# Loading wv in whole rows between the x chunks, both halves of V per row block, and first statistics on two engines

## The chip, the cores and the metric

The kernel runs on one core of a Trainium2 chip. The metric is the device time of one execution in microseconds, about 1.25 us more than the span from the first to the last instruction in its trace (795.23 against 794.0 in the profiled run of the kernel before). Each run also comes with the mean clock that TensorE was granted over its span; here this matters more than usual, since a clock of 0.998 over 795 us is some 1.6 us, and the whole effect of the change is smaller than that.

Engines are named as in the profile: PE is TensorE's matmul, PEld its weight load, DVE VectorE, ACT ScalarE, POOL GpSimd, SP SyncE, which issues the loads.

## The reference, cut to what matters

```python
x = A_x                                         # 2048 x 1024, bf16
h = x + A(layernorm(x), wq, wk, wv, wo, beta)   # attention with a memory, in 4 segments of 512 rows
out = h + B(layernorm(h), w_in, w_sp, b_sp, w_out)
# first thing in A:  v = layernorm(x) @ wv      (1024 x 1024 weights), then q and k the same way
```

The change touches only the first 22 of some 794 us: layernorm of the first 512 rows (four chunks of 128), their transposes, and the first 56 matmuls of `v`.

## The kernel before

Operations are collected in a program; a list scheduler with its own cost model then fixes the order on every engine but TensorE, whose order is that of the source. The parts that matter:

```python
LOAD = "12ab3h"          # x1, x2, wv rows 0-3 left half, rows 4-7 left half, x3, wv right half
START = 'T00 t01 v00 v01 v02 v03 t10 T11 v04 v05 v06 v07 v10 ... v27 u00 u01 ... u27 v30 ... v37'
# Tci / tci: transpose half i of x chunk c on TensorE, copy out of PSUM by VectorE (T) or ScalarE (t)
# vci / uci: matmul of chunk c with row block i of wv, left (v) or right (u) half of the columns
...
def wv_rows(a, b):       # half rows: 512 columns of bf16, 1 KB each
    dma(WV[:, a:b, 0:512], A_wv.rearrange("(c p) n -> p c n", p=128)[:, a:b, 0:512])
...
for k in range(N_WARM):  # 11 matmuls on zeros while the first loads are under way
    mm(PS[:, 7, :], ZERO[:, 0:128], ZERO[:], True, True)
...
def layernorm_act(src, dst, junk, k):            # chunk 1: both statistics on ScalarE, all 1024 columns
    e.activation(junk, src, Identity, scale=-1/D, accum_out=nm)
    e.activation(junk, src, Square, bias=nm, accum_out=ss)
    ...
# chunks 0, 2, 3: two bn_stats of 512 columns each on VectorE, bn_aggr,
# then for all: square root on ScalarE, reciprocal and normalising on VectorE
```

The softmax here doesn't subtract the row's maximum and nothing guards it: scores larger than these inputs give would overflow.

## Time and profile before

| | kernel before |
|---|---|
| time, median of the first 3 runs | 795.27 us (795.21 to 795.57) |
| span of the profiled run | 794.0 us, clock 1.000 |
| TensorE busy | 782.5 us |
| first matmul of V | 8.24 us |
| first matmul of Q (wq) | 21.29 us |

The two last rows are start times counted from the start of the span.

The prediction below shows the waits, the chain and TensorE's timeline. What the other engines do up to the first matmul of V is in their timelines (start, duration, engine, line, operation, output and input; in brackets the idle time and what ended it):

```profile
5.13 1.06 ACT L585 ACTIVATE hx<-xin 128x1024 bf16<-128x1024 bf16 x1
...
6.31 1.15 ACT L587 ACTIVATE hx<-xin,mv 128x1024 bf16<-128x1024 bf16 x1
6.58 0.42 DVE L485 COPY xnT<-ps 128x512 bf16<-128x512 bf16 x1
...
7.79 0.58 ACT L473 ACTIVATE xnT<-ps 128x512 bf16<-128x512 bf16 x1
```

ScalarE does the two full-width statistics of chunk 1. The first copy of chunk 0 out of PSUM is done by VectorE and ends at 7.00; from there on the first matmul lacks only its weights, which land at 8.20.

### The profile page before, as it was taken

The numbers are of one execution on the slowest core, as the hardware profiler recorded it, in microseconds if no ns is written. First come the engines' busy times: TensorE is split into PE (matmuls) and PEld (weight loads), VectorE is DVE, ScalarE is ACT, GpSimd is POOL, SyncE is SP. The second block draws the span as 40 slices with busy tenths as digits, with TensorE's granted clock in tenths as the row PEclk, the third lists the DMA queues.
The fourth block names the chain that finished last, engine by engine and source line by source line (L and its number), as shares of the span: only waits on it lengthen the run. The fifth ranks groups of instructions, "written<-read, shape, count | busy, mean of one in ns | idle before, by whom it ended". The sixth has DMA issues, their size and how long they took to land.

```text
span 794.0 us, 11952 instructions
## 1 busy us (share of the span) xinstructions
PE 782.5 (99%) x5273; PEld 321.4 (40%) x4765; DVE 369.3 (47%) x854; ACT 290.7 (37%) x342; POOL 138.9 (17%) x266
## 2 busy tenths in 40 slices
PE   8999999999999999999999999999999999999999
PEld 3455554555554542341322314443244334423433
DVE  6784687868766686804215051132223222322222
ACT  5778887787878852132323323100000000000000
POOL 0454543444433431200001010000000000000000
PEclk9999999999999999999999999999999999999999
DMA  9756612732333657610000116703410530012001
GB/s 282 189 128 159 149 42 67 144 84 55 72 82 103 161 134 211 159 40 1 1 0 1 26 35 156 188 1 68 119 33 1 119 100 1 0 54 61 0 1 53
DMA packets 129526, 65.02 MB, mean 82 GB/s; under 512 B 96576, under 2 KB 121408, under 8 KB 129472
## 3 DMA queue, kind: packets, MB, share of 16 engines
q1 hardware_dynamic: 129472, 64.25, 32.4%
q8 instruction: 39, 0.64, 0.3%
q14 instruction: 15, 0.12, 0.1%
HBM read 32.51 MB, written 8.39 MB: 52 GB/s over the span
## 4 chain that ended last, share of the span: by engine, by line
PE 96%; DVE 1%; issue 1%; DMA 1%; ACT 0%; SPq 0%; POOL 0%
PE ps L327 78%; PE ps L328 15%; PE ps L464 3%; DMA wv<-in_A_wv_dram 1%; ACT e L473 0%; DVE stats L570 0%; SPq L516 0%; DVE hx L495 0%; DVE pkt L498 0%; DVE xin L489 0%; PE ps L468 0%; DVE oq L495 0%; DVE v L485 0%; POOL e L700 0%; POOL ra L505 0%
## 5 line engine op out<-in xcount | busy, mean ns | idle before, releaser
L327 PE MATMUL ps<-wspT,z 128*128 128x512 bf16 x878 | 193.1, 379 | 0.9
L473 ACT ACTIVATE e<-ps 128x2048 bf16<-128x2048 f32 x80 | 149.8, 1873 | 35.1 <-PE ps L464 35.1
L327 PEld LDWEIGHTS ps<-wspT,z 128*128 128x128 bf16 x896 | 87.7, 98 | 106.4 <-issue 1.0
L473 ACT ACTIVATE z<-ps 128x512 bf16<-128x512 f32 x120 | 63.1, 571 | 145.4 <-PE ps L327 140.5
L495 DVE TENSOR_TENSOR tg<-ps,brow 128x512 bf16<-128x512 f32 x56 | 38.7, 691 | 150.0 <-PE ps L327 121.9
L327 PE MATMUL ps<-hnT,win 128*128 128x512 bf16 x438 | 96.7, 379 | 0.5
L700 POOL TENSOR_SCALAR_AFFINE_SELECT e<-e 128x1024 bf16<-128x1024 bf16 (+1 forms) x80 | 77.4, 968 | 112.2 <-ACT e L473 111.8
L328 PE MATMUL ps<-win,hnT 128*128 128x512 bf16 (+1 forms) x381 | 90.0, 343 | 0.5
L570 DVE BATCH_NORM_STATS2 stats<-z 128x6 f32<-128x448 bf16 x64 | 40.1, 627 | 96.8 <-ACT z L473 95.2
L327 PE MATMUL ps<-wout,y 128*128 128x512 bf16 (+2 forms) x243 | 82.4, 367 | 0.0
L328 PE MATMUL ps<-wout,y 128*128 128x512 bf16 x210 | 79.6, 379 | 0.5
L495 DVE TENSOR_TENSOR hx<-hx,ps 128x512 bf16<-128x512 bf16 (+1 forms) x65 | 42.3, 674 | 77.2 <-PE ps L327 76.8
L327 PEld LDWEIGHTS ps<-hnT,win 128*128 128x128 bf16 x448 | 43.9, 98 | 54.1 <-issue 2.0
L327 PE MATMUL ps<-xnT,wq 128*128 128x512 bf16 x250 | 60.3, 380 | 0.4 <-issue 0.2
L327 PE MATMUL ps<-xnT,wk 128*128 128x512 bf16 (+2 forms) x249 | 57.4, 373 | 2.4 <-DVE ra L502 1.9
L327 PE MATMUL ps<-wv,xnT 128*128 128x512 bf16 x239 | 57.1, 379 | 2.4 <-DMA wv<-in_A_wv_dram 1.5
L327 PE MATMUL ps<-wo,oT 128*128 128x512 bf16 x244 | 57.1, 379 | 0.6
L327 PEld LDWEIGHTS ps<-wout,y 128*128 128x128 bf16 x252 | 24.2, 98 | 72.2 <-issue 69.1
L327 PE MATMUL ps<-win,hnT 128*128 128x512 bf16 x122 | 46.2, 379 | 0.0
L327 PEld LDWEIGHTS ps<-win,hnT 128*128 128x128 bf16 x128 | 12.5, 98 | 81.4 <-issue 80.9
L509 POOL TENSOR_SCALAR rs<-mv 128x1 f32<-128x1 f32 x44 | 10.9, 248 | 192.9 <-DVE mv L573 192.9
L327 PEld LDWEIGHTS ps<-v,e 128*128 128x128 bf16 x1280 | 40.1, 96 | 9.8 <-issue 1.7
(72 smaller groups left out, 635.3 us busy)
## 6 DMA issues: line engine op xcount, KB each, us to landing
win<-in_B_w_in_dram SPq DMA_DIRECT2D x6, 1024.0 KB, 5.7
hx<-in_A_x_dram SPq DMA_DIRECT2D x16, 256.0 KB, 3.3
out_dram<-hx SPq DMA_DIRECT2D x16, 256.0 KB, 2.7
hx<-out_dram SPq DMA_DIRECT2D x16, 256.0 KB, 2.6
out_dram<-hx SPq DMA_DIRECT2D x31, 128.0 KB, 1.7
xin<-in_A_x_dram SPq DMA_DIRECT2D x15, 256.0 KB, 5.0
wout<-in_B_w_out_dram SPq DMA_DIRECT2D x2, 1792.0 KB, 11.1
wq<-in_A_wq_dram SPq DMA_DIRECT2D x2, 1024.0 KB, 8.7
```

The costliest lines, as they stand in the source:

```text
L327: return e.matmul(out, lhsT, rhs, start=start, stop=stop)
L328: return e.add_instruction(mybir.InstMatmult(name="I-%d" % (1000000 + o.idx), engine=e.engine, ins=[e.lower_ap(rhs), e.lower_ap(lhsT)], ou ...
L464: G.op(PE, lambda e: e.matmul(o, lhsT, rhs, start=True, stop=True, tile_position=(32 * i, 0)), [lhsT, rhs], [o], n / 2.4 if last else 3.5, ...
L473: G.op(ACT, lambda e: e.activation(o, i, func, scale=scale, **kw), r, [o], ((172 if inps(i) else 224) + n_of(i)) / 1.2 + 26, prio=prio, na ...
L495: G.op(DVE, lambda e: e.tensor_tensor(o, a, b, op), [a, b], [o], vcost(o, [a, b], fast), name="tt", prio=late[0])
L509: G.op(POOL, lambda e: e.tensor_single_scalar(o, i, s, op), [i], [o], 220 if n_of(o) < 8 else 220 + 2.5 * n_of(o), name="pts1", prio=late[0])
L570: G.op(DVE, lambda e, si=si, so=so: e.bn_stats(so, si), [si], [so], (cs + 143) / 0.96, name="bn_stats", prio=late[0])
L700: G.op(POOL, lambda e: e.affine_select(d, d, pat, ALU.is_ge, 0.0, base=0, channel_multiplier=-1), [d], [d], 1270 if j else 640, name="mask")
```

## The change

The intent: bring the first weights in sooner by loading them in small pieces of whole rows (2 KB), between the chunks of x; give TensorE two matmuls per row block and chunk, so that few blocks keep it busy; and split the statistics of chunks 1 to 3 by columns over ScalarE and VectorE, so that the next chunk is ready in time. Two smaller edits go with it: the first copy of chunk 0 out of PSUM moves from VectorE to ScalarE (`T00` becomes `t00`), and `AFTER` now holds chunk 1's first bn_stats back until chunk 0 is normalised. In the cut below, what stands in parentheses sums up code.

```diff
-    ON_ACT = (1,)
-    LOAD = "12ab3h"
-    START = 'T00 t01 v00 v01 v02 v03 t10 T11 v04 ... (left halves, then right halves)'
-    AFTER = [(1, 1, 5)]
+    SPLIT = (0, 384, 512, 512)      # columns of each chunk's statistics on ScalarE
+    LOAD = "1 0:1 1:3 2 3:4 4:5 3 5:6 6:8"     # x1, row block 0, blocks 1-2, x2, ...
+    START = ("t00 t01 u00 u01 v00 u02 v01 T10 T11 v02 u03 v03 u10 u11 v10 v11 v12 u04 v13 v04 u12 u13 v14 v05 v15 "
+             "t20 u05 u14 v06 v16 T21 v20 u20 u21 u06 v21 v22 u15 u16 u22 v17 ... u27 v30 ... v37 ")
+    AFTER = [((1, 'b0'), (0, 'ts'))]
...
-        dma(WV[:, a:b, 0:512], A_wv.rearrange("(c p) n -> p c n", p=128)[:, a:b, 0:512])
+    dma(WV[:, a:b, :], A_wv.rearrange("(c p) n -> p c n", p=128)[:, a:b, :])
...
-    (layernorm_act for chunk 1; bn_stats of all columns for chunks 0, 2, 3)
+    def layernorm_first(c, wa):
+        ... wa columns: mean and sum of squares on ScalarE, written as one more group of bn_stats
+        ... the rest: bn_stats on VectorE; bn_aggr joins them; the tail as before
...
-        if i == 0: vb[x[:2]] = bank()
+        b = PS[:, 2 + 2 * (c % 3) + h, :]       # both halves of a chunk have their own banks
```

The cost model of the scheduler also takes whole-row loads as 8% cheaper.

## The prediction

> **What bounds the kernel now.** I read four views in this order: the page's busy shares, the waits of TensorE, the chain that ended last over the first microseconds, and the engines' timelines up to 26 us. The page first:
>
> ```profile
> PE 782.5 (99%) x5273; PEld 321.4 (40%) x4765; DVE 369.3 (47%) x854; ACT 290.7 (37%) x342; POOL 138.9 (17%) x266
> PE 96%; DVE 1%; issue 1%; DMA 1%; ACT 0%; SPq 0%; POOL 0%
> ```
>
> TensorE is busy for 782.5 of 794.0 us and carries 96% of the chain that ended last. The change does not remove a matmul, so all it can touch is 794.0 - 782.5 = 11.5 us of TensorE idleness, and only the part before attention starts: the diff changes nothing after the first projections of V. The waits and the chain show where in that start TensorE stands still:
>
> ```profile
> PE ps L327 <- DMA wv<-in_A_wv_dram: 1.5, 1, 1.5
> ...
> 2.64 5.56 DMA wv<-in_A_wv_dram
> 8.20 0.05 issue
> 8.24 1.04 PE ps L327 x4
> 9.28 0.45 PE ps L468 x8
> 9.73 2.00 PE ps L327 x9
> 11.73 0.45 PE ps L468 x8
> 12.17 0.22 PE ps L327
> 12.39 0.05 issue
> 12.44 12.49 PE ps L327 x65
> ```
>
> The start waits for the first wv load: issued at 2.64, landed at 8.20. From there on the chain is TensorE alone. The timeline of TensorE says the same, with exact starts:
>
> ```profile
> 5.91 0.89 PE L468 MATMUL ps<-ident,xin 128*128 128x128 bf16 x8
> 8.24 1.04 PE L327 MATMUL ps<-wv,xnT 128*128 128x512 bf16 x4 [1.45 <-DMA wv<-in_A_wv_dram]
> ...
> 12.01 9.44 PE L327 MATMUL ps<-wv,xnT 128*128 128x512 bf16 x42
> 21.29 1.89 PE L327 MATMUL ps<-xnT,wq 128*128 128x512 bf16 x8
> ```
>
> Between 8.24 and 21.29 there are 56 matmuls of V and two groups of 8 transposes. The 43 matmuls from 12.01 to 21.29 give 9.28 / 43 = 0.216 us each; 56 x 0.216 = 12.1, and the two groups take 9.61 - 9.11 = 0.50 and 12.01 - 11.55 = 0.46 us. The sum is 13.05 us, and 21.29 - 8.24 is 13.05 us: once it has begun, this stage has no hole at all. **What can be won is therefore how much earlier than 8.24 the first matmul of V starts, less every new hole.**
>
> **What the Trainium skill says, and whether the trace agrees.**
> "TensorE: Matmul & The Clock Gate", section "Wait — 56ns, not 53.3ns?", gives 215.7 ns from start to start at N = 512; the trace has 216 ns, so the 13.05 us cannot shrink.
> "ScalarE: Activation LUTs", section "What ACT_TABLE_LOAD costs", gives an ACTIVATE as 186 ns + 0.833 ns per column, 93 ns more with a pointer operand. The two statistics of chunk 1 (1024 columns) take 1057 and 1147 ns in the trace against 1039 and 1132: it agrees, so I use it to size the narrower ones.
> "Perfetto Trace Analysis", section "DMA Optimizations", says that pieces under 2 KB have a noticeable overhead and that splitting may let some work start sooner. The trace agrees in direction: half rows of wv and wq (1 KB) moved at 359 GB/s between 10.3 and 13.2 us, and whole rows of x (2 KB) at 392 GB/s between 20.6 and 21.3, 9% more.
> "DMA: Bandwidth & Descriptors", section "Anatomy of one DMA — SWDGE (gpsimd) path", has some 2 us fixed for a DMA on that other path; here the two small pieces of x chunk 0 landed 2.2 and 2.3 us after issue, so small pieces do not come for nothing, but they overlap.
>
> **The change part by part.**
>
> *Loads.* Before, in order: x0 (two halves), x1, x2, wv rows 0-3 left half (512 KB), rows 4-7 left half, x3, right half (1 MB), wq. The issue and landing of each give, for the bytes up to and with it: 512 KB (x1) at 5.1 us, 768 KB (x2) at 5.8, 1280 KB (first wv) at 8.2, 1792 KB at 9.5, 2048 KB (x3) at 10.3, 3072 KB at 13.2. After: x0, x1, row block 0 (256 KB, whole rows), 1-2, x2, 3, 4, x3, 5, 6-7. On the old curve row block 0 lands at 5.8, blocks 1-2 (1280 KB) at 8.2, block 3 (1792 KB) at 9.5. But the old curve was drawn with 1 KB pieces and 512 KB at a time. By the throughput instead: 0.33 MB had moved at 3.5 us, at 370-390 GB/s blocks 1-2 (1.31 MB in all) have moved by 6.1, and with the 1.2 to 1.6 us by which landings trailed the moved bytes before, they land at 7.3 to 7.7; block 3 likewise at 8.8 to 9.1. I take 7.6 and 9.0. The issues themselves cost 0.43 to 0.51 us each; eleven of them end near 6 us, ahead of the data.
>
> *Chunk 0.* Its statistics are untouched (VectorE, done at 5.84), and the transposes start at 5.91 as before. But both copies out of PSUM now go to ScalarE, where chunk 1's statistics over 384 columns stand first: they start at 5.13 as now, take 0.52 + 0.19 and 0.61 + 0.19 us (1057 and 1147 ns less 640 columns x 0.833, and the accumulator reads of 0.19), so they end at about 6.6; the copy of 0.58 ends at 7.2. The first matmul of V then starts at about 7.25, 1.0 us before 8.24. This is the ceiling of the gain.
>
> *New holes.* The first matmul uses block 0; the second needs block 1, 7.6 against 7.47: 0.15 lost. Chunk 1: VectorE takes 640 columns in two pieces (a 512-wide one takes 0.69, so about 0.48 each) from 5.84 to 6.8, aggregation 0.21, square root 0.29 behind the copy on ScalarE until about 7.45, reciprocal 0.16, normalising 0.55: ready at 8.2, and TensorE arrives at 7.6 + 4 x 0.216 = 8.5. No hole. After both transposes (0.48) and one matmul TensorE wants block 3 at 9.2; it is there at 9.0, or up to 0.3 late. From then on each block of 0.7 us of loading is met with five to eight matmuls (1.1 to 1.7 us), so the loads run ahead. Chunk 2 lands near 8.5, its two ScalarE statistics over 512 columns take about 1.7 us, its normalised rows come near 11.7, and TensorE needs them after 21 matmuls near 12.7. Chunk 3 becomes ready near 13.9 instead of 13.4; the wk load hangs on it and lands perhaps 0.5 later than the present 20.6, wanted at 22.2. Neither should hold.
>
> *Sum.* 1.0 ceiling - 0.15 for blocks 1-2 - 0.1 for block 3 - 0.1 for small things later = 0.65 us earlier at the first wq matmul. What follows is bounded by TensorE, whose longest later waits are 0.2 us each, so I let nearly all of it reach the end: 795.27 - 0.65 = 794.6 us. Less work for VectorE and ScalarE (LayerNorm split) earns nothing by itself: they are not what the start waits for after 8.24.
>
> **The rivals.**
> (a) *The next load takes the place of the first.* If landing follows the old curve, block 1 is there at 8.2 and TensorE does one single matmul before it; gain 0.2 to 0.3 us, 795.0. For it: the cumulative bytes up to blocks 1-2 are exactly those of the old first wv load. Against it: larger rows, smaller pieces. I give it a quarter.
> (b) *ScalarE becomes the bound of the start.* It now carries statistics of chunks 1 to 3, three of the PSUM copies, all V evictions and the table load. If the order puts a statistic that waits for its load ahead of a copy, TensorE waits too: loses 0.5 to 1 us, time 795.3 to 795.8. Against it: ScalarE was idle 0.5 to 1.1 us ahead of most V evictions in the present timeline.
> (c) *The gain is lost or doubled later.* The program is ordered by its own list scheduler, with a load cost changed for every whole-row load, so order in the attention stage may shift. From 33.08 to 43.88 us the chain runs over ScalarE, GpSimd and VectorE, where TensorE waited only 0.16 us at its end; an earlier TensorE could meet VectorE still busy, as the x loads for LayerNorm there land at 21.3 whatever V does. This moves the result by up to 0.4 us either way.
>
> **Range and chances.** The ceiling gives 794.3 with nothing lost, rival (a) 795.0, (b) up to 795.8, and (c) plus or minus 0.4. Runs of the kernel before spread over 0.36 us. So 8 in 10 lie between 793.9 and 795.3. Two per cent would be 16 us, more than all idle time of TensorE, so faster by that is out; slower by it would need a disturbance that nothing in the profile points to.
>
> **What would show it.** Right: the first V matmul near 7.25 us with its wait put down to a copy on ScalarE and not to the load; the second soon after 7.6; the first wq matmul near 20.6 instead of 21.29; TensorE's busy time the same within its missing records. Wrong: the first wv piece landing later than 7.2, a hole of over 0.3 us at blocks 1-2 or 3, a TensorE wait for chunk 2's normalised rows near 12.7, a wait for wk near 22, or a first wq matmul that is earlier while the end is not.

## The result, and the profile after

| | before | after |
|---|---|---|
| median, runs of the same rounds | 795.32 us (795.21 to 796.41, 6 runs) | 794.80 us (794.36 to 796.87, 6 runs) |
| ratio | | 0.9994, 95% interval 0.9982 to 1.0007 |

A ratio is the mean time of one kernel's fast runs over that of the other's of the same rounds, so not quite the ratio of the medians. 794.80 lies in the range, 0.2 above the predicted 794.6.

The profiled execution was the one of 796.87 us, and it is not typical. The page of this run starts so:

```profile
span 795.6 us, 12064 instructions
...
PE 790.3 (99%) x5369; PEld 321.2 (40%) x4760; DVE 369.9 (46%) x854; ACT 293.0 (37%) x351; POOL 138.8 (17%) x269
```

TensorE seems busier by 7.8 us with the same program. Most of that is bookkeeping (5369 matmul records in place of 5273: fewer are missing), but not all. In TensorE's timeline the first matmuls take twice as long as they should:

```profile
7.14 0.39 PE L327 MATMUL ps<-wv,xnT 128*128 128x512 bf16 x1 [0.57 <-ACT xnT L477]
8.61 1.89 PE L327 MATMUL ps<-wv,xnT 128*128 128x512 bf16 x4 [1.08 <-DMA wv<-in_A_wv_dram]
10.29 1.06 PE L472 MATMUL ps<-ident,xin 128*128 128x128 bf16 x8
...
22.92 1.89 PE L327 MATMUL ps<-xnT,wq 128*128 128x512 bf16 x8
```

Four matmuls take 1.89 us where four took 1.04 before. The view by stretches gives the reason; behind the bounds and the length of each stretch stand the busy times of PE, PEld, DVE, ACT and POOL, then the granted clock of TensorE, the DMA share and GB/s:

```profile
5.90:8.60 2.70, 1.01 (x9) 0.54 (x9) 1.93 (x6) 1.97 (x5) 0.00 (x0) 0.96 0.99 347
8.60:11.00 2.40, 2.39 (x11) 1.28 (x12) 0.73 (x2) 1.54 (x4) 0.00 (x0) 0.50 1.05 404
11.00:13.20 2.20, 2.20 (x13) 0.89 (x10) 2.09 (x6) 1.22 (x4) 0.00 (x0) 0.82 1.07 374
```

TensorE's clock fell to one half near 8.4 us (0.04 of 2.7 us missing in the first stretch, at half clock 0.2 us) and came back near 11.8, after some 3.4 us. The traces of three runs below, read in the same way, show half clock for 3.4 us (old_stats, 8.4 to 11.8) and twice that, 6.8 us (coarse, 8.8 to 15.6, and old_order, 9.4 to 16.3); the mean clock of this run and of old_stats is 0.998, of the other two 0.996, so in these traces 0.998 means one such stretch and 0.996 two. The hole before it, from the end of the transposes to 8.61 with one matmul in it, let it fall. So the profile that came with the result shows two things at once: a wait for weights (blocks 1-2 were issued at 2.65 and landed 5.92 us later, at 8.57), and half a clock. A second profile of the same kernel (run "again" below) fell at full clock:

```profile
7.23 1.25 PE L327 MATMUL ps<-wv,xnT 128*128 128x512 bf16 x5 [0.26 <-ACT xnT L477]
8.34 0.62 PE L472 MATMUL ps<-ident,xin 128*128 128x128 bf16 x8
8.80 0.78 PE L327 MATMUL ps<-wv,xnT 128*128 128x512 bf16 x2
...
20.44 1.89 PE L327 MATMUL ps<-xnT,wq 128*128 128x512 bf16 x8
```

Here blocks 1-2 landed after 4.6 us, at 7.2, and no matmul waits for weights; the first wq matmul comes at 20.44 in place of 21.29, and the span is 793.1 in place of 794.0.

Sorted by clock, the changed kernel has 10 of 11 runs at full clock, at a mean of 794.68 us (794.36 to 794.87), and the kernel before 24 of 27 in the three batches that list it, at 795.32 us (794.75 to 796.17). The difference is 0.64 us, with a 95% interval of some 0.2 us either way by the spread of these runs, against 0.65 predicted. It is this sorting by clock, over more runs, that shows a gain. The four runs at 0.998 are 796.87 (after) and 796.34, 796.81 and 797.73 (before). Not every long run has a low clock: two runs of the kernel before, 796.00 and 796.17 us, were at 1.000, and what made them long is open.

### The profile page after: what moved, and what is told of

It is laid out like the page before. It is cut to its first block, busy times and chain, and to the rows that moved or that the text cites. A ratio compares the mean times of both kernels' runs of the same rounds, so it can differ in the third digit from the quotient of the medians.

```text
span 795.6 us, 12064 instructions
## 1 busy us (share of the span) xinstructions
PE 790.3 (99%) x5369; PEld 321.2 (40%) x4760; DVE 369.9 (46%) x854; ACT 293.0 (37%) x351; POOL 138.8 (17%) x269
## 4 chain that ended last, share of the span: by engine, by line
PE 98%; DMA 1%; ACT 0%; SPq 0%; issue 0%; DVE 0%
PE ps L327 80%; PE ps L328 15%; PE ps L468 3%; DMA wv<-in_A_wv_dram 1%; ACT e L477 0%; SPq L520 0%; PE ps L472 0%; DVE hx L499 0%
## 5 line engine op out<-in xcount | busy, mean ns | idle before, releaser
L327 PE MATMUL ps<-wout,y 128*128 128x512 bf16 (+2 forms) x252 | 85.8, 367 | 0.0
L327 PE MATMUL ps<-wv,xnT 128*128 128x512 bf16 x251 | 60.7, 384 | 1.6 <-DMA wv<-in_A_wv_dram 1.1
L327 PE MATMUL ps<-xnT,wk 128*128 128x512 bf16 (+2 forms) x264 | 60.8, 374 | 0.0
L327 PE MATMUL ps<-wo,oT 128*128 128x512 bf16 x256 | 58.8, 379 | 0.0
L327 PE MATMUL ps<-win,hnT 128*128 128x512 bf16 x128 | 48.5, 379 | 0.0
```

What stands on the lines that cost most here:

```text
L327: return e.matmul(out, lhsT, rhs, start=start, stop=stop)
```

## The experiments

The full-clock mean beside each result is over runs listed at clock 1.000; "on that chip" is the kernel before in the same batch. Theory A was that the landing of the first weights paces the start; theory B that the clock makes the long runs. The rival named for theory B in the first expectation, a long run at clock 1.000, did not turn up in the changed kernel, but it did in the kernel before (796.00 and 796.17 in the batch of fill2).

**1. again: the changed kernel, unedited**

> The changed kernel once more, unedited, to see its runs and, if it comes, a trace at full clock. Theory A (landing): the gain is the earlier start of V, 8.24 to 7.14 us, less the hole until row blocks 1 and 2 of wv have landed. At full clock the first wq matmul should start near 20.8 us (before: 21.29), the time be 794.6 to 795.0, 0.3 to 0.7 us under the kernel before. Theory B (clock): the run of 796.87 was long because TensorE stood almost idle from 6.4 to 8.6 us and then ran at half clock to about 12; so any run over 796 must show a mean clock under 1.000, and runs at 1.000 all lie under 795.2. Rival: the long run comes from elsewhere, and a long run at clock 1.000 turns up.

Measured: median 794.70 us (794.36 to 794.84, 5 runs, all at clock 1.000); the kernel before on that chip 795.23 at full clock (8 runs), and 797.73 at 0.998 (1 run). So the difference is 0.56 us there. The wq matmul came at 20.44, earlier than expected, because blocks 1-2 landed at 7.2 and not at 8.57: the same program, with the same bytes ahead, sees 1.4 us of spread in this landing.

**2. fill: dummy matmuls in the holes**

```diff
-    START = ("t00 t01 u00 u01 ...
+    START = ("t00 t01 z00 z00 u00 z00 z00 u01 ...      # z00: matmul on zeros, never read
```

> Two dummy matmuls on zeros before the first matmul of V and two after it, 0.43 us each pair, inside the two holes. They compute nothing that is read. Theory B (clock): with the holes half filled no run shows a clock under 1.000 and none is over 795.5; the median stays at 794.8 plus or minus 0.2, since they lie in holes. Theory A: no change of the median either, as long as blocks 1 and 2 land after 7.8 us; if they land sooner, up to 0.4 us slower. Rival: long runs appear at the same rate with the dummies.

Measured: 795.66 us (795.14 to 796.47), all five runs at clock 1.000. No half clock, but 0.9 us slower than expected. The dummies also went into the cost model, and the scheduler then, among other moves, placed ScalarE's table load ahead of the first copy of chunk 2, whose transposes ended just after the table load had begun (13.49 and 13.38 us). ScalarE's timeline and TensorE's of this run:

```profile
13.38 1.28 ACT L838 ACT_TABLE_LOAD   x1
14.67 0.20 ACT L838 ACTIVATE g<-rs 128x1 f32<-128x1 f32 x1
14.78 0.58 ACT L477 ACTIVATE xnT<-ps 128x512 bf16<-128x512 bf16 x1
...
15.41 0.39 PE L327 MATMUL ps<-wv,xnT 128*128 128x512 bf16 x1 [0.84 <-ACT xnT L477]
```

In "again" the copy runs first, at 12.87, and the table load after it. Rival (b) of the prediction, ScalarE as the bound of the start, did not happen in the change but is one misplaced instruction away from it.

**3. fill2: the same dummies, free in the cost model**

```diff
             mm(PS[:, 7, :], ZERO[:, 0:128], ZERO[:], True, True)
+            G.ops[-1].cost = 0.0
```

> As fill, but the four dummy matmuls count as free in the program's own scheduler, so that the order of instructions on all other engines is exactly that of the changed kernel (in fill the table load had moved ahead of the first copy of chunk 2 and TensorE waited 0.84 us for it). Theory B (clock): no run at a clock under 1.000. If the loss in fill came from that order: the median is 794.6 to 795.0 again, 0.7 us under fill. Rival: the dummies themselves cost, then the median stays near 795.6.

Measured: 794.79 us (794.50 to 794.92), all five at clock 1.000; the kernel before on that chip 795.38 at full clock (7 runs), two more at 0.998 (796.34, 796.81). The order of the other engines in its trace is that of the changed kernel, compared instruction by instruction over the first 60 us. So the loss in fill was the order, not the dummies, and four dummy matmuls in the holes cost nothing measurable. That they prevent the half clock is in line with this run but not shown by it alone, since "again" had no such run either; coarse and coarse_fill settle it.

**4. one_row: blocks 1 and 2 as two loads**

```diff
-    LOAD = "1 0:1 1:3 2 3:4 4:5 3 5:6 6:8"
+    LOAD = "1 0:1 1:2 2:3 2 3:4 4:5 3 5:6 6:8"
```

> Row blocks 1 and 2 of wv as two DMAs of 256 KB in place of one of 512 KB; one more issue of 0.43 us. Theory A (landing paces the start): the second matmul of V needs block 1 alone and starts 0.4 to 0.7 us earlier, the next two then wait for block 2; the time falls by 0.1 to 0.3 us to about 794.6. Rival (completion, not bytes): landings trail by a fixed 1.2 to 1.7 us and the pieces share the queue, so block 2 lands 0.4 us later than the pair did, and the time is the same or 0.1 us worse.

Measured: 794.89 us (794.58 to 795.62), no better than 794.70 for "again" in the same rounds. In its trace, which is of its longest run (795.62), block 1 had landed 3.3 us after its issue, so three matmuls ran from 7.02 on, and block 2 only 5.9 us after its own:

```profile
7.02 0.82 PE L327 MATMUL ps<-wv,xnT 128*128 128x512 bf16 x3 [0.47 <-ACT xnT L477]
9.05 0.60 PE L327 MATMUL ps<-wv,xnT 128*128 128x512 bf16 x2 [1.21 <-DMA wv<-in_A_wv_dram]
```

The wait moved to block 2. The rival was right: finer pieces do not help here.

**5. old_stats: the statistics back on one engine per chunk**

```diff
-    SPLIT = (0, 384, 512, 512)
+    SPLIT = (0, 1024, 0, 0)
-    AFTER = [((1, 'b0'), (0, 'ts'))]
+    AFTER = []                 # chunk 1 has no bn_stats then
```

> The statistics back as before: chunk 1 wholly on ScalarE (1024 columns), chunks 2 and 3 wholly on VectorE; loads and order of matmuls as in the changed kernel. If the split is needed for the gain: the two statistics take 1.06 + 0.19 + 1.15 + 0.19 us from 5.25 on, the first copy of chunk 0 ends near 8.4 in place of 7.1, so the first matmul of V comes near 8.4 and the time is 795.2 to 795.6, the gain gone. Rival (landing alone): blocks 1 and 2 land near 8 anyway, so it costs at most 0.2 us: 794.8 to 795.0.

Measured: 796.85 us (795.20 to 798.08): three runs at clock 0.998, two at full clock, 795.20 and 795.85. The first matmul of V came at 7.93, after a wait of 1.6 us for the copy on ScalarE:

```profile
7.93 2.19 PE L327 MATMUL ps<-wv,xnT 128*128 128x512 bf16 x5 [1.56 <-ACT xnT L477]
```

So without the split the small loads gain nothing: at full clock 0.5 and 1.2 us slower than "again" (two runs). And with the longer hole came the half clock in three of five runs.

**6. coarse: loads in large pieces again**

```diff
-    LOAD = "1 0:1 1:3 2 3:4 4:5 3 5:6 6:8"
+    LOAD = "1 2 0:4 4:8 3"          # 1 MB each, whole rows
```

> The loads back to large pieces (x1, x2, wv rows 0-3 as 1 MB, rows 4-7, x3), order of matmuls and statistics as in the changed kernel. Theory A (landing): 1.79 MB must land before the first matmul of V, so it starts at 8.5 to 9.5 us in place of 7.2 and, since the stage has no slack, the first wq matmul comes at 22 us or later at full clock, the time 796 to 796.6. Theory B (clock): TensorE stands still from 6.4 to about 9, so the runs show a clock of 0.998 and lie 1.3 to 2 us higher still, 797.5 to 798.5. Rival (loads hidden): under 795.3.

Measured: 799.55 us (798.01 to 800.33), clock 0.996 in two runs and 0.998 in two. The first matmul of V waits until 10.45, later than expected:

```profile
10.45 2.29 PE L327 MATMUL ps<-wv,xnT 128*128 128x512 bf16 x5 [3.92 <-DMA wv<-in_A_wv_dram]
...
25.96 1.89 PE L327 MATMUL ps<-xnT,wq 128*128 128x512 bf16 x8
```

**7. coarse_fill: the same with twelve dummy matmuls in that hole**

```diff
-             "t00 t01 u00 u01 ...
+             "t00 t01 z00 (12 times) u00 u01 ...
```

> coarse with twelve dummy matmuls on zeros (2.6 us at full clock) in the hole ahead of the first matmul of V. They do no useful work. Theory B (clock): the clock stays at 1.000 and the time is 1.3 to 2 us under coarse, near 796.3, though TensorE executes more. Rival (no clock effect): the same as coarse or slower.

Measured: 798.10 us (796.24 to 798.83), all four runs at clock 1.000. It executes twelve more matmuls and its mean is 1.54 us lower than that of coarse (797.82 against 799.36). Four runs each, which overlap (798.01 in coarse, 798.83 here), would not settle it alone; their clocks and the two traces do. The weights landed as late as in coarse, and what follows is shorter:

```profile
10.56 1.24 PE L327 MATMUL ps<-wv,xnT 128*128 128x512 bf16 x5 [0.85 <-DMA wv<-in_A_wv_dram]
...
23.54 1.89 PE L327 MATMUL ps<-xnT,wq 128*128 128x512 bf16 x8
```

From the first matmul of V to the first of wq it is 12.98 us here and 15.51 in coarse, with the same matmuls, so this difference is the clock: TensorE left without work loses its clock here (four of four runs), and useless work keeps it (four of four). This is the pair that shows theory B. The size expected was 1.3 to 2 us, and the means differ by 1.54; the two traces differ by 2.5, as the profiled run of coarse is one with two stretches of half clock. The absolute time was 1.8 us above what I expected, since the 1 MB piece landed 1 to 2 us later than I had assumed.

**8. old_order: small loads and split statistics, order of matmuls as before**

> Small whole-row loads and the split statistics kept, but the order of matmuls as before: the left half of V of one chunk after the other, then the right half. The left half of chunk 0 then needs all eight row blocks after eight matmuls, and blocks 6 and 7 land at 12.6 to 13.3 us; 48 matmuls and a group of transposes (10.8 us) follow, so the first wq matmul comes at 23.4 to 24 us: 797 to 798, more if the clock drops in the holes. The order of both halves per row block is then what makes the small loads pay. Rival (order does not matter): within 0.4 us of the changed kernel.

The edit puts the string START of the kernel before into the changed kernel. Measured: 799.40 us (799.18 to 799.85), clock 0.996 to 0.998. TensorE's waits up to 30 us:

```profile
PE ps L327 <- DMA wv<-in_A_wv_dram: 2.4, 4, 0.9
```

Four waits for wv, 2.4 us in all, and the half clock on top: together 4 us slower than the kernel before. With one matmul per row block and chunk, TensorE runs ahead of the small loads.

**9. two_queues: the first half of chunk 0 issued by ScalarE**

```diff
-        dma(XIN[tc][:, h * 512:(h + 1) * 512], x2d[...])
+        dma(XIN[tc][:, h * 512:(h + 1) * 512], x2d[...], eng=SP if h else ACT)
```

(The costs in the scheduler's model were set so that the order of all other instructions stayed the same.)

> The changed kernel with the first half of x chunk 0 issued by ScalarE, ahead of its table load, beside the second half from SyncE. Every later load is then issued about 0.46 us sooner; the order of all other instructions is exactly the same. Theory A (landing paces the start): blocks 1 and 2 land some 0.3 us sooner on average, so the runs in which TensorE waited for them gain and the others do not: the highest full-clock runs come down to 794.7, the median falls 0.1 to 0.3 us under the changed kernel's 794.7 to 794.8. Rival (the loads are bound by throughput, not by issue): the time is the same within 0.1. Rival (contention): the halves of chunk 0 land later than 3.0 and 3.5 us, the statistics start later, and it costs 0.1 to 0.3.

Measured: 794.74 us (794.55 to 795.05), all at clock 1.000; the kernel before on that chip 795.36 (9 runs, all at full clock). No gain over the changed kernel. The second rival, contention, is what the trace shows: the halves landed 2.6 and 2.8 us after their issues, not 2.1 to 2.3, and all of chunk 0's work followed later:

```profile
3.58 1.42 DVE L599 BATCH_NORM_STATS2 stats<-xin 128x6 f32<-128x512 bf16 x2 [0.79 <-DMA xin<-in_A_x_dram]
...
6.42 0.62 PE L472 MATMUL ps<-ident,xin 128*128 128x128 bf16 x8 [0.96 <-DVE xin L493]
```

The statistics start at 3.58 in place of 3.06 before, the transposes at 6.42 in place of 5.91.

**10. two_queues_fill: both edits**

> The same with the four dummy matmuls of fill2. If it helps at all: no run at a clock under 1.000 and a median at or under two_queues plus 0.1 us; candidate for the best version, 794.5 to 794.7.

Measured: 794.91 us (794.77 to 795.07), all at clock 1.000. No better version.

**11. before_two_queues: that edit in the kernel before**

> The kernel before with that one edit. Theory A: it waits for the first wv load, issued 0.46 us sooner now (2.18 in place of 2.64), so V starts 0.2 to 0.45 us before 8.2 and the full-clock runs lie at 794.8 to 795.1 in place of 795.2 to 795.4. Since the hole from 6.4 us on gets shorter, runs at a clock of 0.998 become fewer than the 3 in 18 seen so far. Rival (throughput-bound): the same as the kernel before.

Measured: 795.29 us (795.10 to 797.05; the last at clock 0.998), as the kernel before on that chip. In its trace V starts at 7.92, 0.3 us earlier, but chunk 0 and with it chunk 1 are later, TensorE waits for chunk 1's normalised rows at 9.24, and the first wq matmul comes at 21.37. What was won at one wait was lost at the next.

**12. hold_back: all later loads wait until blocks 1-2 have landed**

```diff
+        if c == "1:3":
+            held_for = len(G.ops) - 1
+        # and for every later load, wq and beta:  G.ops[-1].deps.add(held_for)
```

> The changed kernel with every load after row blocks 1-2 held back until blocks 1-2 have landed; order of issue unchanged. The time is not the point (the later loads come some 2 us late, so 796 or more): what is read is when blocks 1-2 land, which was 8.57 and 7.21 us in two executions of the changed kernel, at the same bytes ahead. If landing trails because the loads queued behind share the DMA engines: they land well before 7.0 us, near 6.3 (1.31 MB at 320 to 350 GB/s from 2.2 us on). Rival (the spread belongs to the bytes ahead alone): they land between 7.2 and 8.6 as before.

Measured: one look, 797.21 us (before beside it 795.47), which is not the point. With nothing queued behind them, blocks 1-2 landed 5.0 us after their issue at 2.65:

```profile
SPq L520 <- DMA wv<-in_A_wv_dram: 4.5, 1, 4.5
```

That is the wait of SyncE's queue (total, times, longest); its timeline has the next issue right after it:

```profile
7.62 0.34 SPq L520 DMA_DIRECT2D xin<-in_A_x_dram  x1
```

7.60 us lies inside the range of 7.2 to 8.6 seen with the queue full. So this one execution gives no sign that what queues behind makes the landings late. In the GB/s of this trace by slices of 0.15 us, little moves between 3.05 and 3.95 us (89, 14, 55, 177, 205, 178 in the slices from 3.05 on). A similar dip stands in the other traces, shorter or longer. Why the dip is there and why it varies stays open.

## Why the prediction was right, point by point

**The start of V and nothing else.** In fourteen traces (those that came with the two kernels, and the twelve runs above) I took the span less the start of the first wq matmul:

| run | first wq matmul, us | span, us | difference, us |
|---|---|---|---|
| before | 21.29 | 794.0 | 772.7 |
| again (after, full clock) | 20.44 | 793.1 | 772.7 |
| after (profiled, half clock) | 22.92 | 795.6 | 772.7 |
| fill | 22.11 | 794.8 | 772.7 |
| coarse | 25.96 | 798.6 | 772.6 |
| old_order | 25.66 | 798.3 | 772.6 |
| hold_back | 23.28 | 796.0 | 772.7 |

It is 772.6 to 772.7 us in all fourteen, though the scheduler had put the later instructions of some of them in other orders. So what is won or lost before this matmul reaches the end one to one, and rival (c), which I allowed 0.4 us either way, does not occur in any of them.

**The ceiling of 1.0 us.** Predicted: first matmul of V at 7.25, held by the copy on ScalarE. Measured: 7.14 and 7.23, released by that copy. Right, by the sizes of the narrowed statistics (0.52 and 0.61 us, as worked out). It is a ceiling only for this choice of engines: in old_order, where VectorE makes that copy, V starts at 6.89. Whether that would pay with the new order of matmuls was not tried.

**Blocks 1-2.** Predicted: landed at 7.6, 0.15 us lost. Measured: 7.2 with nothing lost, and 8.57 with 1.1 us lost. The middle was right and rival (a) came true as well, in another execution. What I missed is that this landing is a spread and not a number: in the seven traces with the same loads ahead of it, it came 4.6, 4.8, 5.0, 5.0, 5.1, 5.6 and 5.9 us after the issue (again, fill2, old_order, hold_back, fill, old_stats, after). The faster movement that I had counted on is there: between 8.6 and 11.0 us whole rows moved at 404 GB/s, where the kernel before moved 368 in the same stretch. The spread shows in the times too: the full-clock runs spread over 0.5 us, and this is the only wait that differs that much between the two profiles, though I have no trace of each run to tie them.

**Chunk 1, block 3 and the rest.** Predicted no hole at chunk 1, 0.1 at block 3, 0.1 later. In "again" the first five matmuls and the transposes of chunk 1 follow each other with no wait listed, and from 7.23 to 20.44 there are 13.21 us where dense work takes 13.05 by the kernel before: holes of 0.16 us in all, against 0.35 in my sum.

**The sum.** 20.6 predicted for the first wq matmul, 20.44 measured in a lucky execution; the mean of the full-clock runs, 794.68, less 1.25 and less 772.7, is 20.7. The gain at full clock is 0.64 us, predicted 0.65; the mechanism was right, but a match to 0.01 us is luck, since the measured difference is known only to some 0.2 us, and one of my terms, 0.15 us for blocks 1-2, was 0 in one execution and 1.1 in another.

**The clock.** I did not think of it, and in a single run it can be the larger effect: 1.5 us between the means of coarse and coarse_fill. In the run of 796.87 the first wq matmul comes 2.48 us later than in "again"; some 1.2 us of it is the late landing (the second matmul of V at 8.61 in place of 7.45), the other 1.3 us is the time from there on, mostly the clock. Which run it meets looks like chance (one in eleven of the same kernel; the last section says what the skill has on it). Both kernels have a hole in which this can happen: 3 of 27 runs before, 1 of 11 after; the counts are too small to say that the change lowers the risk.

**Which part earns it.** None of the three parts can be left out: with large loads the kernel is 4 us slower than before (coarse), and still 2.4 us at full clock (coarse_fill); with the old order it is 4 us slower too (old_order, half clock included), and with the old statistics no faster (old_stats). So each part removes a wait that the other two leave. No run puts one part alone into the kernel before.

The best version found is the changed kernel itself. fill2 has the same time (794.79 against 794.80) and half-filled holes; in these few runs it is a guard against the half clock that costs nothing measurable, but it was not shown to be needed.

## What to carry to other kernels

When one engine has no hole after a certain instruction, follow the start time of that instruction: a change ahead of it is worth what it moves that start, once some traces have shown that the rest keeps its length (here 772.6 to 772.7 us in fourteen). Before using one profile as the picture of a kernel, look at the clock of that run, and at whether a load that paces the start lands at the same time in a second profile. And where a scheduler fixes the order, compare the orders of two versions before putting a difference down to the edit: here an edit of 0.9 us of idle filler moved a table load and cost 1 us.

## What the Trainium skill lacked or had wrong

- "TensorE: Matmul & The Clock Gate", section "Part 1: The HAM clock gate (the "warmup" mystery)", says that TensorE's clock is halved after an idle window of some 3.4 us and comes back after a busy one, that the window runs freely, and it puts the danger at gaps of more than about 3.4 us. The traces agree on the state, 0.50 from about 8.4 to 11.8 us, and with such a window: half clock lasted 3.4 us in two traces and 6.8 us in two. They do not agree on the gap: the clock fell to 0.50 after a hole of some 2 us (6.6 to 8.6 us) that had a matmul in it, and in three of five runs of old_stats, whose profile shows a hole of 1.6 us ahead of the first V matmul. Twelve matmuls on zeros in a hole of 3.9 us kept it at 1.00.
- "DMA: Bandwidth & Descriptors" gives a fixed part and a rate for a DMA issued by GpSimd, but no spread between executions, and the loads here are issued by SyncE: the same 512 KB load, at the same place in the queue, landed 4.6 and 5.9 us after its issue in two executions of one kernel.
- No page gives a figure for what it costs to issue the first loads from two engines at once: two halves of 128 KB landed 2.6 to 3.0 us after issue when issued together from SyncE and ScalarE (three runs), and 2.1 to 2.3 us when issued 0.46 us apart from SyncE alone.
